# Block-sparse attention with a gated FFN on one core: first keys issued ahead of the constants, the first FFN products split, more zero matmuls at the start, and a new order of all work

## The chip, the cores and the metric

The kernel runs on one core of a Trainium2 chip. The metric is the device time of one execution in microseconds (us), the lower the better. Times are given as the median of several runs; the profile is one further execution, with its own time beside its span from the first to the last instruction. In the text PE is TensorE (PEld its weight loads), ACT ScalarE, DVE VectorE, POOL GpSimd and SP SyncE.

## What is computed

Attention over 4 batches, 8 heads, 768 tokens of 64 values, with a mask of 32 x 32 blocks: the neighbouring blocks, the first and last block row and column, and three sampled blocks per block row. Its output, 3072 tokens of 512 values, goes through a gated feed-forward layer. Cut from the reference:

```python
scores = scale * np.matmul(q, k.transpose(0, 1, 3, 2))
mask = np.abs(blk_i - blk_j) <= window
mask = mask | (blk_i == 0) | (blk_j == 0) | (blk_i == n_blocks - 1) | (blk_j == n_blocks - 1)
for qb in range(n_blocks):
    for kb in sampled_blocks[qb]:
        mask[qb * block:(qb + 1) * block, kb * block:(kb + 1) * block] = True
scores = np.where(mask, scores, -1000000000.0)
...
attn = attn / (np.sum(attn, axis=-1, keepdims=True) + 1e-09)
x = np.matmul(attn, v)      # as (3072, 512)
gate = 1.0 / (1.0 + np.exp(-(x @ w_gate)))
out = gate * (x @ w_val) @ w_out
```

## The kernel before

**Tiling.** A unit is 256 query tokens of one batch: 12 units, three per batch. In a unit the heads go in four pairs, and each pair in three steps of 256 keys. A step is a score (matmuls of kT and qT, 64 rows each, the two heads side by side on the two halves of TensorE's rows), an exp on ACT from PSUM to the tile P (128x1024), and a multiplication of P by the mask on DVE. A pair's value product, PV, multiplies P with the values, which carry a column of ones, so that the row sums come out with it (24 matmuls of 128 rows in the first two units, 48 of 64 rows later); DVE then takes the reciprocal and writes the normalized x. x is turned into xT, in the first two units by TensorE and a copy, later by a DMA transpose on SP's queue.

**FFN.** Units are grouped: the first four groups are one unit each (256 tokens), the later four two each (512). An FFN job computes one PSUM slot full of the gate's and the value's products over four chunks `c` of 128 values, one chunk for each pair of heads; ACT takes a tanh of the gate half, DVE multiplies into `ht`. In the one-unit groups a group has six jobs. Then `y` multiplies `ht` with w_out in parts of four `f` each, and the output goes through a copy and an SP DMA.

**The head.** The first unit's masking is done by adding: extra matmuls of `bias` and the spread matrix `e64` go into each score's PSUM sums, in place of the DVE multiplication. The mask needs the sampled block numbers (`mask_blocks`, task 0), spread by a matmul to rows (tasks 1 to 4; task 2 writes `bias`, task 4 `mb24`), and mask tiles made from `mb24` by matmuls and copies. The first pair's keys and queries are loaded as f32 into `k32` and `q32`, cast on ACT or DVE, transposed by TensorE (tasks 5 to 13: keys in two pieces, 5 to 7 and 8 to 10, and queries, 11 to 13) and copied to `kT` and `qT`. The other pairs' first keys, queries and values, the rest of the queries, and all weights are cast by DMA on POOL's queue in the order of `FIRST`, one after another. Tasks 30, 32 and 34 are the first pair's three scores. The zero matmuls (`idle`, from the tile `junk`) are pairs that read zeros and write a PSUM slot.

**What sets the order.** The schedule is manual. Each piece of work is a task of `Plan` with its engines, estimated costs and dependencies. `Plan.run` goes through the string ORDER: a token is a task's number, with a letter for the engine where there is a choice, `:n` for one of four PSUM slots (each two banks, tiles `m0` to `m3`) that the task takes, and `@n` to let a load wait for a score. `j3` is a pair of zero matmuls into slot 3. The order in the string is the order on every engine and queue; waits come from the data dependencies. Tasks are numbered as they are added, so most numbers after the first FFN job differ between the two kernels.

**Lines** of the profile: L247 and L252 to L257 the first DMAs, L220 and L230, L235 loads and weights, L280 and L282 copies on ACT and DVE, L315 zero matmuls, L338 nearly all matmuls, L397 spread rows, L451 and L456 TensorE transposes, L411 the bias, L570 exps, L576 masks, L615 and L616 the norm, L667 xT transposes by DMA, L762 and L765 tanh and gate.

Of the kernel before, what the change touches and what calls it, by code (L numbers as in the profile page):

```python
# [12 lines left out]
f16 = mybir.dt.float16  # L13
f32 = mybir.dt.float32
# [27 lines left out]
23D 25:3 27:2 37 26D 215@30 50:1 28D 46:3 51 82:2 48:0 83D 47 64:1 49 84:2 60:0 85D 65 38:3 29 61  # L42
56:2 39 66:1 57 42:0 67D 54:3 43D 52:1 165:0 53D 55 93:2 24 58:1 166 94 99:3 59 68:2 95:0 100 96D
181:1 69D 62:0 182 63D 78:3 102:2 162:0 79D 144@102 103 70:1 126:3 125@50 71D 183 163 164 111:1
127 119:2 131:0 120 128 167 112 104 138:3 122:2 132 145:1 123 133 121 139 124 169:0 146 140 147
72:2 170 86:3 159:1 73D 87 171 152:2 160 205:0 153 108:3 88 89:1 206 105@89 90 101 174:2 92@165
154 109 187@89 207 239:1 91 235@86 175 155:0 188:3 110 156 114@40 176 168@155 240 113 115:0 157
189 141:2 116 202:1 142 190 195:0 203 143 196 232:3 172:2 233 129:0 173 97:3 191:2 130 204 192A
193 98A 117:0 256 212:2 194 216 118A 213 184:3 177:0 217 178A 185 134:2 148:0 218 149D 135D 241
242:0 198:3 221A 252:2 214 199 136 179 219A 258 180 246:3 200 253 227 137 254 268:1 247 257 243  # L50
248 150 229:2 234 151 269 209:3 300:0 210 270 259 161 230 237 197 293:1 296:3 228 301 284:2 231
297 302 238 244 294 280:0 186 287:3 285 201@280 211 281 286 249:1 298 288 277:0 223:2 289 278 250
224 251 336:3 327:0 337 158@336 225 274 264:1 279 261:2 271:3 265 295 236 328 262 266 272 310:1
329 273 311 226 263 307:2 320:3 255 340 308 290 312 303:1 321 309 323:2 341 282 324 333:3 208 304
378@333 322 342 334 305 347:2 345A 343D 351:3 314:1 245@351 352 348 338 372:0 315 299@64 349 373
365:3 316 357@181 369 375:2 353 386:0 403@239 358:1 376 317 374 366 387 377 325 354:2 359 367 355
368 404:0 360 356 432:3 400:2 405 433 361 313@400 260 393:1 326@307 401 335 411:3 267@333 406 402
418:2 394 419 424@418 412 407 283@138 395 362:0 413 389:2 379:1 390 414 363 397:3 425:2 364 398
# [3 lines left out]
442:3 385 448 493:2 457A 451 455A 443 371 516:1 465 494 517 444 507:0 429 430 495 518 459:3 490:1  # L62
# [3 lines left out]
532:2 644:0 551 533 529:1 645 534 597:2 562 530 646 563 557 598 594:0 564 578 392@594 595 531  # L66
601:1 633@421 565D 567A 561@32 627:2 569:0 610 628 573:3 579@141 570 602 438@122 571 574 629
339@555 630:2 587:0 631 596 704@50 647:3 575 588 548@397 603 648 604 600@470 580:2 396 683@209 589
662:1 545:3 581 668@165 663 590 632 619:0 546 622:1 664 582 599 620 611:3 623 583 612 621 615:2
624 665:3 625 673:0 666 616 547 350 674 756:1 614@40 634:3 675 757 710 695 584:0 553 617 635 445  # L70
718@435 618 651:1 636 535@662 585 650@102 680:2 652 586 681 637 684:0 653 613 677:2 701:3 654 685
# [3 lines left out]
739:0 727 733 679 731 743:3 740 744 734 741 755 688:1 752 735A 722:0 728 689 737A 723 690 787:3  # L75
749:2 788 724 801:1 572 742 798:0 745 790:3 750 799 748 709 751 791 766:0 541 802 792 769:3 759
770 711 772:1 767 760 773 768 676 844:3 779:0 761 775:1 762A 764D 845 780 763 818:2 776 781 800
# [6 lines left out]
906 916 885 912 909A 921:1 913 974 946 922 924 927 923 907D 970:3 941:2 900 931 971 901:0 942 972  # L84
918:3 932 917 919 933 902 947:2 934D 954:3 936A 975 903 959:0 965:1 960 943 948 961 955 949 966
# [6 lines left out]
1067:0 1065 1081 1068 1085 1069 937 1066 1070 1086 935 1074 910 1075 1087 1076 1090D 1100:3 1091  # L92
1079D 1096:0 1077D 1078 1101 1080 1097 1102 1132:2 1103 1098 1088A 1108:3 1099 1089 1120:1 1109
1112:0 1110 1121 1111 1113 1122 1092:3 1123 1114 1124:1 1115 1133 1093 1104:0 1094 1125 1095 1105
1126 1134 1136:3 1127 1106 1135 1116:1 1107 1128:2 1117 1137 1118 1129 1119 1138 1140:0 1139 1130
1141 1131 1142 1150:1 1151 1152 1143 1153 1144 1154 1145 1160:3 1146A 1148D 1161 1147 1162 1149
1155:2 1163 1156 1164 1157 1158 1159
# [23 lines left out]
class Plan:  # L121
# [33 lines left out]
def kernel(  # L155
# [30 lines left out]
    const_np = np.zeros((128, 128 + 8 * NB), np.float16)  # L186
    const_np[:, 0:128] = np.eye(128)
    const_np[0:NB, 128:] = mc_np.reshape(NB, 4 * NB).view(np.float16)
    const_h = nc.inline_tensor(const_np, name="bb_const")
# [10 lines left out]
    const = sing.tile([128, 128 + 8 * NB], f16)  # L200
    ident = const[:, 0:128]
# [38 lines left out]
    mc = const[0:NB, 128:].bitcast(f32).rearrange("a (n c) -> a n c", c=4)  # L240
# [11 lines left out]
    nc.sync.dma_start(const, const_h.ap())  # L252
# [3 lines left out]
    nc.gpsimd.dma_start(e64[0:NB], spread_h.ap())  # L256
    nc.scalar.dma_start(e64[D : D + NB], spread_h.ap())  # L257
# [55 lines left out]
    def idle(unit):  # L313
# [789 lines left out]
```

## Time and profile before

| | us |
|---|---|
| median of 3 runs | 283.81 (283.0, 283.81, 402.41) |
| profiled execution | 281.96 |
| its span | 280.2 |
| exps on ACT (144) | 142.5 busy, 1.025 each |
| mask multiplications on DVE (132) | 86.7 busy, 0.686 each |
| FFN gate and value matmuls (2 x 672) | 136 busy for each of the two, side by side |
| PV matmuls (2112) | 48.2 busy |

The page gives busy time and counts by engine, the span in 40 slices, the DMA queues, the chain that ended last, and the costliest groups of instructions. Matmuls overlap in TensorE's pipeline, so their busy time is longer than the time between two starts. In the timeline a row gives start, length, engine, line, operation, tiles and count, with the idle time in front of it and what ended it in brackets. The mean granted clock of the profiled execution is 0.994 of full speed.

### The profile page before, as it was taken

To read this page: it belongs to the slowest core of one execution; us is meant where nothing else is said; L and a number is where in the kernel's file an instruction comes from. 1 tells how busy PE (TensorE), PEld (TensorE's weight loads), DVE (VectorE), ACT (ScalarE), POOL (GpSimd) and SP (SyncE) were. 2 spreads that over 40 slices of the span, in tenths; PEclk is the share of its full clock that TensorE was granted. 3 is DMA by queue.
4 is the path that set the end of the run, shared out by engine and by line. 5 is a ranking of instruction groups with operands and counts; after the bars stand their busy time and mean duration, and the time that the engine had idled before them with its cause. 6 is when DMAs were issued, how large, how long until landed. Compare 5 with 4: busy or idle time off the path is not lost.

```text
span 280.2 us, 10875 instructions
## 1 busy us (share of the span) xinstructions
PE 272.4 (97%) x4889; PEld 186.1 (66%) x4889; DVE 187.9 (67%) x387; ACT 192.1 (69%) x239; POOL 47.4 (17%) x70
## 2 busy tenths in 40 slices
PE   5999999999999999999999999999999999999995
PEld 2677786777899799766555655666656667555543
DVE  4667894788887888688778746875664888142421
ACT  3798888699897878898668866578677683023301
POOL 8975441011531000082400000000000000000000
PEclk9799999999999999999999999999999999999999
DMA  7999999765589975279967330041100012440003
GB/s 148 184 195 196 200 205 202 110 127 87 77 110 150 206 129 126 40 106 188 125 115 162 68 97 2 12 133 50 30 2 0 6 21 65 117 180 2 0 5 147
DMA packets 56679, 28.92 MB, mean 103 GB/s; under 512 B 33044, under 2 KB 53676, under 8 KB 56632
## 3 DMA queue, kind: packets, MB, share of 16 engines
q0 software_dynamic: 21552, 13.93, 35.6%
q1 hardware_dynamic: 34592, 13.99, 22.7%
q8 instruction: 38, 0.62, 0.9%
q10 hardware_dynamic: 488, 0.30, 0.4%
q14 instruction: 9, 0.07, 0.1%
HBM read 28.47 MB, written 6.29 MB: 124 GB/s over the span
## 4 chain that ended last, share of the span: by engine, by line
PE 91%; DMA 3%; ACT 2%; DVE 2%; issue 1%; SPq 0%; DVEq 0%
PE m L338 89%; DMA xT<-x 2%; DMA e<-bb_spread 1%; ACT P L570 1%; PE m L456 1%; DVE ysb L833 1%; ACT ysb L831 0%; PE m L451 0%; DVE kT L282 0%; DVE mask L282 0%; ACT mask L280 0%; SPq L667 0%; PE m L397 0%; DVE x L616 0%; PE m L315 0%
## 5 line engine op out<-in xcount | busy, mean ns | idle before, releaser
L570 ACT ACTIVATE P<-m 128x1024 f16<-128x1024 f32 x144 | 142.5, 1025 | 31.3 <-PE m L338 27.3
L338 PE MATMUL m<-xT,wv 64*128 64x512 f16 (+2 forms) x672 | 136.1, 331 | 0.3 <-issue 0.3
L338 PE MATMUL m<-xT,wg 64*128 64x512 f16 (+2 forms) x672 | 135.9, 331 | 0.1
L576 DVE TENSOR_TENSOR P<-P,mask 128x1024 f16<-128x1024 f16 x132 | 86.7, 686 | 11.1 <-ACT P L570 10.8
L338 PEld LDWEIGHTS <-wg 64*128 64x128 f16 (+1 forms) x672 | 61.8, 94 | 20.5 <-issue 2.0
L338 PEld LDWEIGHTS <-wv 64*128 64x128 f16 (+1 forms) x672 | 61.8, 94 | 15.9 <-issue 0.3
L338 PE MATMUL m<-wo,ht 64*128 64x512 f16 (+2 forms) x564 | 70.7, 372 | 0.0
L765 DVE SCALAR_TENSOR_TENSOR ht<-th,m 128x512 f16<-128x512 f32 x72 | 49.0, 686 | 30.6 <-ACT th L762 29.6
L762 ACT ACTIVATE th<-m 128x512 f32<-128x512 f32 x72 | 42.7, 598 | 36.0 <-PE m L338 35.3
L338 PE MATMUL m<-qT,kT 64*128 64x256 f16 x576 | 54.0, 272 | 0.3 <-DVE ysb L833 0.2
L338 PEld LDWEIGHTS <-P 64*128 64x128 f16 (+1 forms) x2112 | 46.2, 94 | 9.0 <-issue 1.1
L338 PE MATMUL m<-vex,P 64*128 64x65 f16 (+1 forms) x2112 | 48.2, 190 | 0.0
L338 PEld LDWEIGHTS <-ht 64*128 64x128 f16 (+1 forms) x564 | 30.5, 94 | 21.6 <-issue 1.3
L338 PEld LDWEIGHTS <-kT 64*128 64x128 f16 x576 | 27.4, 95 | 13.0 <-issue 1.7
L220 POOL DMA_DIRECT2D v<-in_v_dram x16 | 11.4, 717 | 65.3 <-PE m L338 56.5
L616 DVE TENSOR_TENSOR x<-m,rz 128x256 f16<-128x256 f32 x48 | 20.4, 425 | 1.7
L615 DVE RECIPROCAL rz<-m 128x4 f32<-128x4 f32 x48 | 8.7, 180 | 17.9 <-PE m L338 16.4
L220 POOL DMA_DIRECT2D q<-in_q_dram x19 | 13.6, 723 | 12.1 <-PE m L338 11.1
L831 ACT ACTIVATE ysb<-m 128x512 f32<-128x512 f32 x13 | 7.5, 597 | 10.6 <-PE m L338 9.9
L833 DVE TENSOR_SCALAR ysb<-m 128x512 f32<-128x512 f32 x9 | 6.1, 688 | 11.8 <-ACT ysb L831 5.5
L220 POOL DMA_DIRECT2D k<-in_k_dram x15 | 10.8, 723 | 6.1 <-PE m L338 5.5
L338 PE MATMUL m<-bias,e 64*128 64x256 f16 x48 | 6.9, 301 | 0.3
(46 smaller groups left out, 69.7 us busy)
## 6 DMA issues: line engine op xcount, KB each, us to landing
out_dram<-ysb SPq DMA_DIRECT2D x23, 256.0 KB, 2.4
v<-in_v_dram POOLq DMA_DIRECT2D x16, 192.0 KB, 5.5
k<-in_k_dram POOLq DMA_DIRECT2D x15, 192.0 KB, 5.9
q<-in_q_dram POOLq DMA_DIRECT2D x12, 192.0 KB, 7.1
wg<-in_moe_w_gate_dram POOLq DMA_DIRECT2D x6, 256.0 KB, 8.6
wv<-in_moe_w_val_dram POOLq DMA_DIRECT2D x6, 256.0 KB, 8.9
wo<-in_moe_w_out_dram POOLq DMA_DIRECT2D x3, 512.0 KB, 12.8
xT<-x SPq DMA_TRANSPOSE x40, 3.2
```

Source lines behind the costliest of these rows:

```text
L220: return nc.gpsimd.dma_start(dst[:, h0:h1, t0:t1, :], src[b, h0:h1].rearrange("h (p t) d -> p h t d", t=NT)[:, :, t0:t1, :],)
L338: return nc.tensor.matmul(out, lhsT, rhs, start=start, stop=stop, skip_group_check=True).ins
L456: nc.tensor.transpose(out16[a * D : (a + 1) * D, h, i * D : (i + 1) * D], tile_[rows, a], ident[rows, rows],)
L570: nc.scalar.activation(self.pt.rearrange("a h i n -> a (h i n)"), both(self.bank).rearrange("a h n -> a (h n)"), AF.Exp, bias=0.0, scale=SCALE
L576: nc.vector.tensor_tensor(self.pt, self.pt, m.unsqueeze(1).broadcast_to([128, 2, 2, UQ]), op=ALU.mult,)
L615: nc.vector.reciprocal(rz, self.acc[:, :, :, D : D + 1])
L616: nc.vector.tensor_tensor(self.x16.rearrange("a s h d -> a h s d"), self.acc[:, :, :, 0:D], rz.broadcast_to([128, 2, 2, D]), op=ALU.mult,)
L762: nc.scalar.activation(th, both(bank)[:, 0, :], AF.Tanh, bias=0.0, scale=0.5)
L765: nc.vector.scalar_tensor_tensor(self.ht[:, tiles[0] : tiles[-1] + 1, :], in0=th.rearrange("a (f n) -> a f n", n=self.w), scalar=1.0, in1= ...
L831: nc.scalar.activation(ysb, both(bank)[:, s, :], AF.Copy, bias=0.0, scale=0.5)
L833: nc.vector.tensor_scalar(ysb, in0=both(bank)[:, s, :], scalar1=0.5, scalar2=None, op0=ALU.mult)
```

## The change

Four things.

1. The constants. Identity and block table were one tensor `const` (128 x 320, 80 KB), loaded first on SP's queue. They become `ident` (128 x 128, 32 KB) and `mc` (24 x 24 x 4, f32, 9 KB). SP's queue issues now keys, identity, and the spread rows for partitions 0 to 23; ACT's queue block table, sampled blocks, queries; POOL's queue first the spread rows for partitions 64 to 87.
2. The first two jobs of the first group's FFN are two tasks each: chunks 0 to 2, which wait for three pairs' xT, and chunk 3, which waits for the fourth's.
3. Zero matmuls: tokens `j1s` and the like are pairs with 128 columns instead of 512. The head has 10 wide pairs and 4 narrow ones; it had 8 wide ones.
4. ORDER is new from beginning to end: the order of all tasks, their PSUM slots, the engines of the copies with a choice, and the scores that the loads wait for. The first pair's keys are cast by ACT (first piece) and DVE (second), its queries by ACT; task 32 is the first score instead of task 30; the mask tiles come after it.

```diff
+EARLY = 2
 ORDER = """
-j3 j3 j3 j3 0 j3 j3 j3 11D 1:0 8A 3:1 5D 12:2 6:3 4A 7D 2 13A 80:3 106:1 9:0 30:2 107A 10D 81D
-15:1 31 34:0 16D j3 76:3 17:2 35 32:1 18D 77D 74:2 33 40:0 14 20:3 75D 41 44:1 21D 22:2 45 19 36:0
...
+j3 j3 j3 j3 0 j3 j3 j3 5A 8D 1:0 j1 11A 6:1 2 j2s 9:2 12:3 3:0 10D 13A 7A j2s 32:2 4D j3 15:3 33
+j1s 78:1 34:0 16D 79A j3s 80:3 30:2 81D 35 17:1 18D j3 76:3 31 20:1 77D 40:0 21D 22:3 41 36:2 19
+97:1 23D 37 44:0 98D 50:3 45 27:1 46:2 28D 25:1 51 48:0 26D 24 47 54:1 49 74:3 55 75D 60:0 64:2 14
+61 66:3 58:1 67D 65 56:3 59 117:0 57 118D 86:1 89:2 29 68:0 90 38:3 69D 87 93:0 39 62:2 52:3 94
+102:1 63A 103 42:2 53D 95:0 43D 108:3 96D 111:2 109 70:0 104 126:1 71D 112 110 119:3 88 140:0 127
+120 113 132:2 128 141 129 130:3 72:1 131 122:0 133 91 147:3 134 73D 123 135 142 84:1 99:2 148
...
             if token[0] == "j":
-                self.idle(int(token[1:]))
+                self.idle(int(token[1]), 128 if token[2:] else 512)
...
-    const = sing.tile([128, 128 + 8 * NB], f16)
-    ident = const[:, 0:128]
+    ident = sing.tile([128, 128], f16)
...
-    mc = const[0:NB, 128:].bitcast(f32).rearrange("a (n c) -> a n c", c=4)
+    mc = sing.tile([NB, NB, 4], f32)
...
-    nc.sync.dma_start(const, const_h.ap())
+    nc.scalar.dma_start(mc, mc_h.ap())
     nc.scalar.dma_start(sbi, sampled_blocks)
     first_heads(nc.sync, k32, k, 0, NT)
     first_heads(nc.scalar, q32, q, 0, 2)
-    nc.gpsimd.dma_start(e64[0:NB], spread_h.ap())
-    nc.scalar.dma_start(e64[D : D + NB], spread_h.ap())
+    nc.sync.dma_start(ident, ident_h.ap())
+    nc.sync.dma_start(e64[0:NB], spread_h.ap())
+    nc.gpsimd.dma_start(e64[D : D + NB], spread_h.ap())
...
-    def idle(unit):
+    def idle(unit, n):
         for i in range(2):
             nc.tensor.matmul(
-                units_ps[unit][:, i, :],
+                units_ps[unit][:, i, 0:n],
                 junk[i * D : (i + 1) * D, 0:128],
-                junk[i * D : (i + 1) * D, :],
+                junk[i * D : (i + 1) * D, 0:n],
...
+            if self.g == 0 and j < EARLY:
+                a = plan.add(
+                    [(PE, 1.5 * F_HALF)],
+                    half(None, range(3)),
+                    xdone[0][:3] + before("ht", 0),
+                    take=bank,
...
+                a = plan.add(
+                    [(PE, 0.5 * F_HALF)],
+                    half(None, range(3, 4)),
+                    [a] + xdone[0][3:],
...
-            if self.ns[-1] < WIDE:
+            elif self.ns[-1] < WIDE:
```

In the new order task 126 is the first part of the first FFN job and task 103 the exp that uses its PSUM slot before; 63 is the copy of a pair's xT that ACT makes, 79 a mask tile's copy on ACT, 70 transposes of later queries. In the old order task 126 is the first FFN job whole.

More of the change, by code (lines that the diff above doesn't have):

```diff
@@ L45 @@
[L45 to L56, printed above, removed]
@@ new lines @@
+270:1 139 216 221A 236 223A 153 202 167:3 271 231:2 229 302:0 232 181 239 230 272 168 233 197:2
+241:1 182 169 254:3 198 195 303 196 199 260 248:2 255 304 240 242 258 256 259 266:0 243 249 251:1
+225:3 267 250 252 261 226 253 106:2 273:0 107A 227 309:1 276 274 310 114@309 207:2 275 312:3
+247@46 208 313 292 295:0 286:1 209 296 268 297 263:3 287 279:2 289:0 203@263 238 264 288 160@143
+280 228 265 298:1 290 329:3 299 291 325:2 330 163 326 281 322:0 282:1 314 331 323 262 305:2 283
+300 356:0 342 311 357 338:1 257 343 327 339 353:0 284 344 354 380@353 210 306 359@143 347D 345A
@@ new lines @@
+391:1 367:0 269@56 392 307 316:3 324 328@36 335:2 402:1 340 317 341@99 336 368 318 405@183 403 337
+420:2 332 381:3 358 369 364:1 421 319 370 382 393 365 383 349:0 366 413:2 384 350 399:1 427:3 351
+400 426@399 404 374:0 394@399 414 355 375 315@244 401 437:1 428 415 285@30 422 438 360:0 301@122
+416 429 448:1 444:2 430 449 361 277 406:3 376 362 432 465:1 363 445 433 466 407 446 395:0 333 224
+408 434:1 371 441:2 435 409 396 293 385 377:3 439 442 378 320 472:1 222 397 443 321 473 379 388:3
+423:0 467 454 389 278 455 424 390 334 451:1 450 518:3 410:0 452 436 456 417 425 519 478:1 308 457A
@@ new lines @@
+453 411 479 459A 412 475:3 431 461:2 480 482:0 476 481 462 483 463 468:1 485:3 469 484 471 521:2
[4 rows of a table added]
+398 533 557:3 597 566 589:2 558 567D 571:1 569A 562 610:3 590 352 611 559 616@108 603:0 591 580
+706@30 632:3 592 572 440@30 633 604 598 670@560 586:2 573 605 652@46 621:3 587 606 635@50 700:1
+622 701 588 624:0 550@560 623 685@157 629:2 682:1 582:3 630 581@231 625 537@489 683 631 613:2 634
+583 626 684 614 617:1 627 584 703:2 664:0 585 618 665 447 636:3 612 720@282 704 653:0 563@89 619
+602@231 599:2 620 637 600 555 717:1 712 556 654 638 615 718 639 657:2 570 666 655 675:3 667:1 656
[4 rows of a table added]
@@ new lines @@
+751:2 791 729 752 730 745:1 753 662 746 644 698 820:3 645 736 821 761 595 739D 731:1 737D 784:3
+732 833 748:0 762 747 749 733 771:1 785 772 776 800:0 822 763 786 773 801 813:1 750 766A 856:0
+764D 814 767 787 663 857 815 768:2 858 810:3 699 769 816 792:0 811 770 793 777:1 740 757 803:2
[4 rows of a table added]
+889 861 900:2 920:3 678 906 901 864 849:0 890 921 907 893 850 917:2 908 913:3 911A 909D 897:0 914
+918 848 923:1 851 898 915 903:2 924 904 899 869:3 932 916 972:0 964:2 919 925 973 926 905 870 965
+946:0 902 933 947 871 940:2 974 887 961:3 934 962 922 1018:0 941 1006:3 935 1019 942 960 953:2
@@ new lines @@
+1007 936D 967:0 938A 937 954 1049:3 939 968 955 1050 971 1021:1 995:2 1022 956:3 969 1031:1 970
[6 rows of a table added]
+1078 1089 1081D 1102:3 1079D 1080 1094:0 1106:1 1095 1107 1096 1090A 1103 1097 1092D 1098:0 1104
+1093 1108 1114:2 1105 1082 1099 1115 1100 1118:3 1101 1116 1109 1126:0 1117 1110:1 1122:2 1111
+1119 1112 1127 1113 1120 1123 1128 1130:1 1129 1124 1121 1134:0 1125 1138:3 1135 1139 1136 1131
+1137 1140 1142:2 1141 1132 1143 1133 1144 1157:0 1145 1146 1147 1162:3 1150A 1163 1148A 1151 1158
+1091 1164 1149 1159 1165 1152:1 1160 1166 1161 1153 1154 1155 1156
@@ L185 @@
     )
[L186 to L189, printed above, removed]
+    ident_h = nc.inline_tensor(np.eye(128).astype(np.float16), name="bb_ident")
+    mc_h = nc.inline_tensor(mc_np, name="bb_blocks")
     spread_h = nc.inline_tensor(e24_np, name="bb_spread")
@@ L355, in turns, with whole @@
                 )
-    def whole(mms, bank):
+    def whole(mms, bank, begins=True, ends=True):
         for n, job in enumerate(mms):
@@ L361, in whole @@
                 out, lhsT, rhs = job(g, slice(0, 128))
-                bank.last = tiled(out, lhsT, rhs, n == 0, n == len(mms) - 1)
+                bank.last = tiled(
+                    out, lhsT, rhs, begins and n == 0, ends and n == len(mms) - 1
+                )
     copies = {}
@@ L740, in f, with half @@
             tiles = range(self.per * j, self.per * (j + 1))
-            def half(first):
+            def half(first, cs=range(4)):
                 def go(eng):
@@ L745, in go @@
                     for o, f in enumerate(tiles):
-                        for c in range(4):
+                        for c in cs:
                             mms.append(
@@ L754, in go @@
                     if first is None:
-                        whole(mms, bank)
+                        whole(mms, bank, cs[0] == 0, cs[-1] == 3)
                     else:
@@ L774, in f @@
             deps = xdone[self.g] + before("ht", self.g)
-            if self.ns[-1] < WIDE:
+            if self.g == 0 and j < EARLY:
[4 more added lines that the diff above has]
+                    take=bank,
+                    ops=12 * self.per,
+                    wide=True,
+                )
+                a = plan.add(
+                    [(PE, 0.5 * F_HALF)],
+                    half(None, range(3, 4)),
+                    [a] + xdone[0][3:],
+                    ops=4 * self.per,
+                    wide=True,
+                )
+            elif self.ns[-1] < WIDE:
                 a = plan.add(
```

27 lines of the change are left out of this document (4 added, 23 removed), and 39 rows, old and new, of the table ORDER.

## The prediction

> **What bounds the kernel now.** I read the page first, then busy time by stretches, then the head in the timeline and the DMA issues.
>
> ```profile
> PE 272.4 (97%) x4889; PEld 186.1 (66%) x4889; DVE 187.9 (67%) x387; ACT 192.1 (69%) x239; POOL 47.4 (17%) x70
> ```
>
> TensorE is busy 97% of the span, so only the work that it waits for, or does slowly, can be gained. The stretches say where that is (busy us and count for PE, PEld, DVE, ACT, POOL, then the granted clock and DMA):
>
> ```profile
> 0.00:10.00 10.00, 6.74 (x81) 3.36 (x81) 4.87 (x16) 5.00 (x7) 8.55 (x16) 0.92 0.92 156
> 10.00:20.00 10.00, 9.65 (x226) 7.00 (x226) 6.89 (x17) 8.73 (x10) 8.15 (x12) 0.91 1.41 195
> 20.00:30.00 10.00, 9.77 (x170) 7.17 (x165) 7.33 (x18) 9.17 (x12) 6.07 (x9) 1.00 1.45 195
> ...
> 240.00:250.00 10.00, 10.00 (x96) 5.46 (x94) 3.19 (x6) 1.58 (x3) 0.00 (x0) 1.00 0.50 173
> ```
>
> Busy time overlaps in the pipeline, so I count by pitch, from start to start in the timeline: 0.108 us for a 64x512 matmul (two run side by side), 0.109 for 128x256, 0.0545 for 64x256, 0.015 for 64x65, 0.030 for 128x65. By these, the work that starts before the first FFN matmul (25.02) is 12.0 us: 13.0 are lost there. From 25.02 to 50.23, where the second group's FFN begins, work is 23.4 of 25.2: 1.85 lost. From 50.23 to the last output tiles (269.64) only 3.6 of 219.4 are lost. The gain is to be sought in the head.
>
> What paces the head is ScalarE's chain of exps. Timeline of ScalarE and, by single microseconds, the clock:
>
> ```profile
> 5.28 0.62 ACT L280 CAST qp<-kp 128x512 f16<-128x512 f32 x1 [3.26 <-DMA kp<-in_k_dram]
> ...
> 8.08 1.02 ACT L570 ACTIVATE P<-m 128x1024 f16<-128x1024 f32 x1
> 9.55 1.02 ACT L570 ACTIVATE P<-m 128x1024 f16<-128x1024 f32 x1 [0.45 <-PE m L338]
> 11.41 7.67 ACT L570 ACTIVATE P<-m 128x1024 f16<-128x1024 f32 x8 [0.84 <-DVE mask L282]
> ...
> 22.78 3.77 ACT L570 ACTIVATE P<-m 128x1024 f16<-128x1024 f32 x4 [0.20 <-PE m L338]
> ```
> ```profile
> 8.00:9.00 1.00, 0.88 (x32) 0.74 (x32) 1.00 (x3) 1.00 (x2) 1.00 (x2) 0.72 1.37 188
> 9.00:10.00 1.00, 1.00 (x10) 0.33 (x6) 0.23 (x1) 0.55 (x2) 0.99 (x2) 0.50 1.40 190
> ...
> 11.00:12.00 1.00, 1.00 (x14) 0.67 (x10) 1.00 (x3) 0.58 (x1) 1.00 (x3) 0.58 1.41 174
> ```
>
> The first exp starts at 8.08; the 15th ends at 24.72 and frees the PSUM slot that task 70's transposes take, and behind them the first FFN matmul stands (25.02). Fifteen exps at 0.96 (8 in 7.67) are 14.4 of these 16.6 us; ScalarE stood idle 2.0, of which 1.3 (0.45 and 0.84) in a stretch, 8.44 to 11.84, in which the granted clock was 0.5 and pairs of 64x256 came 0.21 apart instead of 0.11.
>
> **Keys in front of the constants.**
>
> ```profile
> kp<-in_k_dram SPq DMA_DIRECT2D x1, 384.0 KB, 4.1
> ...
> kp<-in_q_dram ACTq DMA_DIRECT2D x1, 128.0 KB, 4.0
> ...
> const<-bb_const SPq DMA_DIRECT2D x1, 80.0 KB, 2.0
> e<-bb_spread POOLq DMA_DIRECT2D x1, 36.0 KB, 4.0
> ```
>
> The keys were issued at 1.15 and landed at 5.25; now they take SyncE's first place (0.74): 4.85. The queries go from ScalarE's second place to its third (1.40 to 1.86, where that queue issued its third DMA before). Their landing lies between 5.4, as now, if the bytes in flight set it (the 80 KB constant gives way to 41 KB), and 5.86 by their own 4.0. The block numbers move from 0.77 to some 1.4, which delays the mask blocks (done 3.66) to 4.3, still before anything that needs them. The spread rows for partitions 0 to 23 go behind the identity on SyncE: between 3.6 (issue 1.6 and the constant's 2.0) and just behind the keys, 5.3; the half that stays on GpSimd landed at 5.58 and keeps its place. GpSimd's later loads move past nothing.
>
> The first score now: query cast on ScalarE (0.38 to 0.48), four transposes (0.2), query copy 0.38 beside the mask-row matmuls (three, 0.59), four bias and four key matmuls (0.62 to the last end): 1.6 after the queries, 7.0 to 7.5. I take 7.2; outer bounds 6.9 and 7.7. The key path (DVE cast 0.68, transposes 0.3, bias 0.41, copy 0.42) is done by 6.7, under it.
>
> **The head to the first FFN matmul.** Its slot is freed by the 15th exp again, task 103, but in the chain stand now a mask copy (0.59), which was done ahead of the first exp, and an xT copy (0.38), which DVE did. 7.2 + 15 x 0.96 + 0.06 + 0.97 = 22.6, matmul at 22.65: 2.35 earlier. This takes ScalarE as never idle. Scores cost TensorE 0.44 per exp, some 0.25 of transposes and masks beside: under 0.96 at full clock. The loads allow it: the last keys and queries of the head landed by 12.8, needed at about 15. If ScalarE keeps half of its old idle, 1.0 is lost again.
>
> **First FFN jobs in two parts.** The same 16 matmuls; the first 12 need three pairs instead of four. The fourth pair's transposes stand ahead of them in the new order anyway, so this hides at most one copy (0.29) and a 0.4 matmul tail; it is in the 22.65. Behind the second part's wait for that copy stands the second job, but the copy ends under the first part's 1.3.
>
> **Zero matmuls.** 16 become 20 of 512 columns and 8 of 128: two pairs at 0.216 and four at some 0.055 more, 0.65 in all. They lie in waits for ScalarE, and cost nothing while those last; without the cover 0.65, at half clock 1.3.
>
> **FFN and weights.** From the first FFN matmul to the third part of the first y stand, in the new order, six FFN jobs (10.5), two y parts (1.7), 12 scores (2.6), four PVs (2.8) and 0.45 of transposes and a mask: 18.1, so 40.9 with 0.2 of waits. The weights come by GpSimd's queue at the old times, as DMA runs at 195 GB/s without a break: the last wv (issued 24.01, 9.8) at 33.8, needed at 34.8; the third wo (27.98, 13.5) at 41.5, needed at 40.9. TensorE waits 0.6 there. With these two waits and 0.1 after, 0.9 is lost from the first FFN matmul to the second group's, against 1.85: a gain of 0.95. The next batch's keys and queries (first one issued at 28.96, landing in 13.4) have about 1.4 to spare.
>
> **The other orders.** ScalarE, DVE and the matmul count stay; after 50 us the 3.6 lost can fall to 2 or rise to 6. At two places the new order leaves 4.3 and 4.5 us of TensorE work between a pair's last PV matmul and the FFN job that reads its xT (at some 116 and 202 us), where 6.05 was the least: 0.3 for both. Sum: 2.35 + 0.95 - 0.3 = 3.0. The profiled execution took 281.96, 280.2 of it span: 277.2 and 279.0. The runs before have 283.0 and 283.81 beside a stray 402.41; from the median, **280.8**.
>
> The half clock lasted from 8.44 to 11.84 (shares 0.72 and 0.58 of its first and last microsecond), and the longest idle time of TensorE ahead of it was 0.8. [...]
>
> **Rivals.** (1) The half clock comes in spite of the fillers. For it: it came when TensorE was busy 38 to 91% of each microsecond from 5 to 8, and from 4.85 to about 5.6 it will be idle still. Against: fillers stand now between the transposes. Price: ScalarE's 1.3 us of idle time return: 282.1. Chance 0.2.
> (2) The first score comes no earlier: queries and spread rows land where they did or later, as they stand third. Price: the 0.9, 281.7. For: keys and queries landed within 0.2 of each other. Chance 0.1.
> (3) Slower: xT lands too late at the two short places. From PV to issue it takes 0.75 (DVE's 0.18 and 0.42 with gaps), from issue to landing 3.2 in the median, 5.9 at most (SyncE's xT transposes). It decides from 3.6. At 5.9 both stall by 2.3: with the 0.3 returned, 285.1. For: 5.9 occurs, where loads are in flight. Against: in the new order the last batch's loads go only after the first of these jobs, and none is left at the second; the median suffices. Chance 0.09.
> Forecast 0.58; 0.03 for what I don't see.
>
> **Numbers.** Low end: gain of 3.0, and 1.6 off the later losses, and the runs' 0.8 spread: 278.4. High: rival 1, with 1.7 of new losses later: 283.8; rival 3 is left out. Two per cent, 5.7 us, is about what a measurement of this kernel can tell from no change: faster by that needs 278.1 or less, 0.07; slower by that needs rival 3 with more places than two, 0.03; within, 0.9.
>
> **What would show it.** First exp at 7.2 (6.9 to 7.7), ScalarE without idle time to 22, clock 1.00 from 5 to 30, first FFN matmul at 22.65, a wait for wo near 41, equal losses after 50. A clock of 0.5 near 9 is rival 1; waits of TensorE near 116 and 202 for xT are rival 3. I am wrong if the losses after 50 us grow by more than 2.

## The result, and the profile after

The change made the kernel slower: 287.57 us in the median of its runs (285.51 to 291.94) beside 283.81 of the kernel before, a ratio of 1.0131 with a 95% interval of 1.0095 to 1.0167. That is under the 2% that a single comparison is trusted with, so "no change by 2%" was right, but it is a loss, and the forecast was a gain: 280.8, with a range that ended at 283.8. One run of each kernel (402.41 before, 291.94 after) was in a slow state, and the ratio leaves both out.

The profiled execution after took 286.93, 285.2 of it span. I count "lost" time as in the prediction: span less the work that starts in it, by its pitch (zero matmuls are no work). The work is the same in both kernels, so the totals, 27.06 for 22.09, differ by as much as the spans do, and the table says where:

| | before | after | all four repairs (e10) |
|---|---|---|---|
| first exp starts | 8.08 | 8.93 | 7.79 |
| first FFN matmul | 25.02 | 25.77 | 24.50 |
| lost up to 50 us | 14.71 | 15.64 | 14.34 |
| lost 50 to 100 | 2.06 | 5.16 | 2.85 |
| lost 100 to 270 | 1.61 | 1.90 | 2.07 |
| lost 270 to the end | 3.70 | 4.35 | 3.74 |

The page's line of engines and, with one row added, the same stretches in the profile after (busy us and count for PE, PEld, DVE, ACT, POOL, then the granted clock and DMA), and behind them the added stretch in the profile before:

```profile
PE 274.3 (96%) x4901; PEld 190.9 (67%) x4901; DVE 187.5 (66%) x387; ACT 190.8 (67%) x239; POOL 47.4 (17%) x70
```
```profile
0.00:10.00 10.00, 7.39 (x77) 3.79 (x79) 3.93 (x14) 3.76 (x6) 8.62 (x17) 1.00 0.93 155
10.00:20.00 10.00, 9.36 (x221) 6.89 (x218) 6.81 (x16) 9.04 (x11) 8.15 (x12) 1.00 1.41 195
20.00:30.00 10.00, 9.65 (x195) 7.67 (x192) 7.70 (x19) 9.33 (x12) 5.18 (x7) 1.00 1.45 197
83.00:93.00 10.00, 7.75 (x176) 7.37 (x172) 6.85 (x15) 6.73 (x8) 3.52 (x5) 1.00 0.91 133
240.00:250.00 10.00, 10.00 (x158) 5.77 (x154) 2.75 (x7) 0.09 (x1) 0.00 (x0) 1.00 0.36 81
```
```profile
83.00:93.00 10.00, 9.72 (x234) 8.50 (x228) 8.00 (x18) 8.29 (x10) 2.28 (x4) 1.00 1.10 147
```

The surprise is the fourth row: from 83 to 93 us, deep in the steady part, TensorE is busy 7.75 of 10 us (9.72 before). The clock of 1.00 in the first row is not to be believed: the first clock record of this execution is at 11.09, and pairs of 64x256 stand 0.21 apart until then and 0.11 behind it, as at the granted 0.50 and 1.00 of the profile before: half speed.

**The head.** DMA issues of the first 9 us, then ScalarE's timeline, both after:

```profile
kp<-in_k_dram SPq DMA_DIRECT2D x1, 384.0 KB, 3.2
kp<-in_q_dram ACTq DMA_DIRECT2D x1, 128.0 KB, 4.6
```
```profile
4.00 0.40 ACT L280 CAST qp<-kp 128x256 f16<-128x256 f32 x1 [1.99 <-DMA kp<-in_k_dram]
6.54 0.40 ACT L280 CAST qp<-kp 128x256 f16<-128x256 f32 x1 [2.13 <-DMA kp<-in_q_dram]
...
8.93 1.02 ACT L572 ACTIVATE P<-m 128x1024 f16<-128x1024 f32 x1 [0.95 <-PE m L338]
10.25 0.58 ACT L280 CAST mask<-m 128x512 f16<-128x512 f32 x1 [0.30 <-PE m L338]
11.11 1.94 ACT L572 ACTIVATE P<-m 128x1024 f16<-128x1024 f32 x2 [0.27 <-PE m L338]
13.48 10.42 ACT L572 ACTIVATE P<-m 128x1024 f16<-128x1024 f32 x11 [0.44 <-PE m L338]
24.09 0.37 ACT L280 COPY xT<-m 128x256 f16<-128x256 f16 x1 [0.18 <-PE m L453]
24.50 2.85 ACT L572 ACTIVATE P<-m 128x1024 f16<-128x1024 f32 x3
```

The keys did land earlier (3.98 for 5.25), but the queries, now third on ScalarE's queue, were issued at 1.90 and landed at 6.51 (5.41 before). The first exp starts 0.85 later than before. From there to the end of the 15th exp it takes 16.59 us, as before (16.64): of the old 2.0 of idle time 0.95 is now filled by the mask copy and the xT copy, and the rows' brackets still leave 1.2.

**The new gaps.** TensorE's timeline after at 61 us, and the chain that ended last (start, length, what) near 85 and 92; then the one such row of TensorE's timeline before:

```profile
60.65 0.37 PE L338 MATMUL m<-vex,P 64*128 64x65 f16 x13
61.58 0.70 PE L338 MATMUL m<-vex,P 64*128 64x65 f16 x35 [0.56 <-issue]
```
```profile
85.09 0.61 ACT th L764
85.70 0.89 issue
86.59 5.27 PE m L338 x128
91.86 0.65 issue
92.51 2.49 PE m L338 x62
```
```profile
83.83 0.27 PE L338 MATMUL m<-xT,wv 64*128 64x256 f16 x1 [0.28 <-issue]
```

At 61 TensorE stops in the middle of one PV's products, and "issue" means that it waited for nothing that the profile shows. At 85 the profile puts the first part of the stop down to a tanh (85.09 to 85.70) and only the 0.89 behind it to "issue". The tanh did not hold the score, though: in e5 below, which has the same order of work, the same score starts ahead of that tanh:

```profile
84.58 0.40 PE L337 MATMUL m<-qT,kT 64*128 64x256 f16 x4
```
```profile
84.75 0.60 ACT L763 ACTIVATE th<-m 128x512 f32<-128x512 f32 x1
```

So the whole stop, from 84.72 to 86.59, has no cause on another engine that the profile shows. Between the stops at 85 and 92 lie exactly 128 matmuls (`x128`). Each matmul comes with a weight load (4901 of each on the page), so 128 matmuls are 256 instructions. The page has a DMA queue that fits: 38 packets of instructions with 0.62 MB, 16 KB each, and 2 x 4901 TensorE instructions are 38.3 times 256. By these counts the packets carry TensorE's own instructions, 256 in each, and the three gaps (0.72, 1.76 and 0.81 above the pitch, 3.3 together; before there is one of 0.44, at 83.3) stand where it steps from one such block into the next. When the block for the stop at 85 came, the DMA answers for the stretches 80.7 to 83.4 and 83.4 to 84.9 of the kernel after tell (packets, MB, share of 16 engines):

```profile
q0 software_dynamic: 517, 0.37, 93.6%
```
```profile
q0 software_dynamic: 17, 0.01, 6.4%
q8 instruction: 1, 0.02, 5.9%
```

TensorE entered the block in hand at 80.66. In the 2.8 us behind it the queue of the key, query and value loads (q0) held the 16 DMA engines for 93.6% of the time, and no instruction packet moved; the one packet came at 83.48 to 84.89, and TensorE went on at 86.59. The loads in flight here are a burst of six, issued 0.7 apart at 73.98 to 77.58, the last of which landed at 85.79. A second burst of five, at 83.33 to 86.11, lies over the next block: TensorE entered that one at 86.59, its packet moved 3.69 later (90.28 to 91.25), and the stop at 92 followed.

**The end.** The last step of the chain before, then after:

```profile
277.00 0.42 DVE ysb L876
```
```profile
281.45 0.69 DVE ysb L894
```

The new order puts the full 128x512 output last, before it was a half tile. From the last matmul's end to the span's end it takes 3.75 for 3.24.

### The profile page after: what moved, and what is told of

Its sections match the earlier page's. It is cut to its first block, busy times and chain, and to the rows that moved or that the text cites. A ratio compares the mean times of both kernels' runs of the same rounds, so it can differ in the third digit from the quotient of the medians.

```text
span 285.2 us, 10906 instructions
## 1 busy us (share of the span) xinstructions
PE 274.3 (96%) x4901; PEld 190.9 (67%) x4901; DVE 187.5 (66%) x387; ACT 190.8 (67%) x239; POOL 47.4 (17%) x70
## 4 chain that ended last, share of the span: by engine, by line
PE 88%; DVE 4%; DMA 3%; ACT 2%; issue 1%; ACTq 0%; DVEq 0%
PE m L338 86%; DMA kp<-in_q_dram 2%; DMA xT<-x 1%; DVE P L578 1%; ACT P L572 1%; PE m L458 1%; DVE x L618 1%; PE m L315 1%; DVE mask L282 0%; ACT th L764 0%; DVE ysb L851 0%; PE m L453 0%; DVE rz L617 0%; DVE ht L767 0%; DVE ysb L894 0%
## 5 line engine op out<-in xcount | busy, mean ns | idle before, releaser
L338 PE MATMUL m<-qT,kT 64*128 64x256 f16 x576 | 55.0, 271 | 1.9 <-ACT th L764 1.6
L338 PEld LDWEIGHTS <-P 64*128 64x128 f16 (+1 forms) x2112 | 45.3, 94 | 7.7 <-issue 0.9
L338 PE MATMUL m<-vex,P 64*128 64x65 f16 (+1 forms) x2112 | 46.8, 190 | 0.6 <-issue 0.6
L338 PEld LDWEIGHTS <-ht 64*128 64x128 f16 (+1 forms) x564 | 31.7, 94 | 20.6 <-issue 1.5
L338 PEld LDWEIGHTS <-kT 64*128 64x128 f16 x576 | 29.0, 95 | 15.8 <-issue 4.3
L851 DVE TENSOR_SCALAR ysb<-m 128x512 f32<-128x512 f32 x10 | 6.7, 688 | 11.2 <-PE m L338 8.4
L849 ACT ACTIVATE ysb<-m 128x512 f32<-128x512 f32 x12 | 6.9, 606 | 6.2 <-PE m L338 5.6
L315 PE MATMUL m<-junk 64*128 64x512 f16 (+1 forms) x28 | 6.7, 515 | 1.8 <-DVE junk L286 1.7
```

Source lines behind the costliest of these rows:

```text
L315: nc.tensor.matmul(units_ps[unit][:, i, 0:n], junk[i * D : (i + 1) * D, 0:128], junk[i * D : (i + 1) * D, 0:n], start=True, stop=True,)
L338: return nc.tensor.matmul(out, lhsT, rhs, start=start, stop=stop, skip_group_check=True).ins
L849: nc.scalar.activation(ysb, both(bank)[:, s, :], AF.Copy, bias=0.0, scale=0.5)
L851: nc.vector.tensor_scalar(ysb, in0=both(bank)[:, s, :], scalar1=0.5, scalar2=None, op0=ALU.mult)
```

## The experiments

All ratios are to runs of the kernel before on the same chip; line numbers shift by a few from kernel to kernel. Theories: *instructions* (the loss lies where TensorE's own instructions arrive late), with *operands* as its rival (the loads' bytes or other waits of the new order hold the work back); and for the head *landing* against *exps* and *clock*.

**e1: fewer instructions.** The PV of all units from the third on with 12 matmuls of 128 rows per half instead of 24 of 64 rows, 960 matmuls fewer in all:

```diff
-            for s in range(2):
+            for s in (0, 1) if first is None else (0,) if first else (1,):
...
-            if first is None:
-                whole(mms, self.bank)
-            else:
-                turns(mms, self.bank, first)
+            whole(mms, self.bank, first is not False, first is not True)
```

> The changed kernel; from the third unit on, each half of a PV is 12 matmuls of 128 rows in place of 24 of 64 rows. Same work at the same pitch by row (0.030 against 2 x 0.015), 960 TensorE matmuls and as many weight loads fewer. Theory A (TensorE waits for its own instructions: 16 KB blocks, 128 matmuls each, that are fetched late while loads of keys and values are in flight): the gaps put down to issue at 61, 85 and 92 us (0.7, 1.8, 0.8) shrink to under 0.5 in sum, and the profiled execution is 2.5 to 3.5 us shorter. Theory B (those gaps are waits for ScalarE, PSUM slots or xT that the new order made): they stay within 0.5 us, the time too.

Measured: 295.26, ratio 1.0428 (1.04 to 1.0456). The gaps at 61, 85 and 92 are gone, which agrees with instructions, yet the time rose. TensorE's timeline in e1 shows why:

```profile
101.06 0.27 PE L338 MATMUL m<-xT,wv 64*128 64x256 f16 x1
101.26 0.54 PE L338 MATMUL m<-vex,P 128*128 128x65 f16 x12
101.73 0.28 PE L338 MATMUL m<-xT,wv 64*128 64x256 f16 x1
```

From the last 64-row matmul to the first of 128 rows it is 0.20 where the pitch is 0.109, and the twelve take 0.47 where twelve pitches are 0.36: 0.09 is lost going in and 0.11 coming out. From 62 to 260 us there are 115 such changes, some 11.5 us at 0.1 each, which is more than the 3.3 of the stops. As a test of instructions by the time this run is spoilt; it measured something else of use, below.

**e2: the loads without their bytes.** The third batch's loads bring 2 of 128 partitions.

```diff
-                lambda eng: load_heads(dst, src, b, 2 * p, 2 * p + 2),
+                lambda eng: load_heads(dst, src, b, 2 * p, 2 * p + 2)
+                if b != 2
+                else nc.gpsimd.dma_start(
+                    dst[0:2, 2 * p : 2 * p + 2],
+                    src[b, 2 * p : 2 * p + 2].rearrange("h (p t) d -> p h t d", t=NT)[0:2],
+                ),
```

> The changed kernel; the loads of the third batch's keys, queries and values bring 2 of 128 partitions only (the rest of that batch's data is left out, so its results are those of other data). All instructions, waits and their order stay. Theory A: the instruction fetches from 70 to 95 us start without delay, the gaps at 85 and 92 us vanish (2.5 us less); the one at 61 us, ahead of most of these loads, may stay. Theory B: the gaps stay.

Measured: 285.07, 1.0059 (1.0032 to 1.0086). The gaps at 85 and 92 are gone, the one at 61, where no such load is in flight, stayed (0.85). The instruction packets themselves show the link: behind TensorE's entry into the blocks ahead of the stops at 85 and 92 they start after 0.10 and 0.16 us in e2, after 2.80 and 3.69 in the change. The loads cause two of the three.

**e3 and e4: the two halves of the change.** e3 is the kernel before with the constants and first DMAs of the change; e4 is the changed kernel with those of the kernel before (part 1 of the change and its reverse).

```diff
...
-    nc.sync.dma_start(const, const_h.ap())
+    nc.scalar.dma_start(mc, mc_h.ap())
     nc.scalar.dma_start(sbi, sampled_blocks)
     first_heads(nc.sync, k32, k, 0, NT)
     first_heads(nc.scalar, q32, q, 0, 2)
-    nc.gpsimd.dma_start(e64[0:NB], spread_h.ap())
-    nc.scalar.dma_start(e64[D : D + NB], spread_h.ap())
+    nc.sync.dma_start(ident, ident_h.ap())
+    nc.sync.dma_start(e64[0:NB], spread_h.ap())
+    nc.gpsimd.dma_start(e64[D : D + NB], spread_h.ap())
```

> The kernel before with the changed kernel's constants and first DMAs alone, old order. If the late queries (landing 6.5 against 5.4) cost what they delay: first exp about 9.0 to 9.2 against 8.08, and 0.8 to 1.2 us slower than before. Rival, that ScalarE's idle time takes it up: within 0.3 of before.

> The changed kernel's order, split products and fillers, with the constants and first DMAs of before. Queries land at 5.4 again: first exp at 7.8 (at half clock) to 7.3 (full clock), the first FFN matmul 1.1 earlier than in the changed kernel (25.8), and the time about 1 us under the changed kernel's; the gaps from 60 to 95 us stay, so it is still 1 to 3 us slower than before. If the late DMAs are the whole cause, it is as fast as before or faster.

Measured: e3 283.93, 1.0043 (1.0014 to 1.0073); e4 286.28, 1.0113 (1.0087 to 1.014). Of 283 us that is 1.2 for the DMAs and 3.2 for the order; together 1.56% where the whole change has 1.31% (0.95 to 1.67). In e3 the queries landed at 6.81 and the first exp started at 9.97 (at half speed until 11.03, which the expected 9.0 to 9.2 left out). In e4 they landed at 5.17, and still the new order won nothing in the head (at half speed until 10.86):

```profile
8.35 1.02 ACT L574 ACTIVATE P<-m 128x1024 f16<-128x1024 f32 x1 [0.95 <-DVE mb L284]
...
12.99 10.38 ACT L574 ACTIVATE P<-m 128x1024 f16<-128x1024 f32 x11 [0.52 <-PE m L340]
```

15th exp done at 25.02, first FFN matmul at 25.26: 0.24 later than before. And the old order is not free of the stops: e3 has 1.05 at 84.8 and 0.80 at 91.0, where the profiled run of before had 0.44 and none.

**e5: the same loads, spread.** Eleven load tokens of ORDER stand behind other scores, most of them 2 to 4 us apart:

```diff
-380@353 ... 359@143 ... 269@56 ... 328@36 ... 341@99 ... 405@183 ... 426@399 ... 394@399 ... 315@244 ... 285@30 ... 301@122
+298:1 269@298 ... 322:0 426@322 ... 338:1 328@338 ... 391:1 285@391 ... 402:1 315@402 ... 420:2 301@420
+... 399:1 380@399 ... 437:1 359@437 ... 448:1 405@448 ... 434:1 394@434 ... 388:3 341@388
```

> The changed kernel with the eleven loads of the third batch behind other scores of the second unit, about 2 us apart and each from about 7 us earlier to 11 us later than now; all bytes are still brought, and nothing else moves. Instruction theory (TensorE's own next 16 KB of instructions wait behind five loads issued 0.7 us apart): the two gaps at 85 and 92 us (1.76 and 0.81) shrink below 0.5 together while the one at 61 us (0.72) stays; time 287.57 - 2.2 = about 285.3. Load theory (the bytes themselves, wherever they are put, hold TensorE's operands back): the 2.5 us only move with the loads; time 287 to 288, the gaps at other places and in front of matmuls that wait for a tile.

Measured: 284.58, 1.0082 (1.0053 to 1.0112). The stretch of 83 to 93 us in e5:

```profile
83.00:93.00 10.00, 10.00 (x241) 9.17 (x238) 8.38 (x18) 8.42 (x11) 2.80 (x4) 1.00 0.82 88
```

TensorE is busy all 10 us (7.75 in the change) with all bytes brought; the gaps at 85 and 92 went together and came nowhere else (lost from 80 to 100: 0.24 for 2.71), the one at 61 stayed at 0.87. That is instructions against operands. The burst matters, not the bytes: in the change six and then five loads of 192 KB were issued 0.7 apart, in e5 two of the eleven stand that close and the rest 2.0 to 4.2 apart. The instruction packets of the two blocks start 1.66 and 1.79 behind TensorE's entry, between the 0.1 to 0.2 of e2 and the 2.8 to 3.7 of the change, and that is soon enough.

**e6: the run of PVs broken up.** In the change eight PV halves stand almost back to back at 59 to 61 us, and 128 matmuls are used up in 2.24 us. One FFN job (286) goes in between:

```diff
-... 253 106:2 273:0 107A 227 309:1 276 274 310 ... 295:0 286:1 209 ...
+... 253 227 106:2 286:1 107A 287 276 273:0 288 274 309:3 310 ... 295:0 209 ...
```

> The changed kernel with the run of eight products with the values at 59 to 61 us broken up: one FFN job (16 long matmuls) is put in front of the last four, and the scores behind take other banks. Instruction theory: 128 matmuls there take 4 us instead of 2.24, so the gap of 0.72 at 61 us goes; the gaps at 85 and 92 stay; time 286.5 to 287.0. Rival (the gap at 61 is the fill of the products' pipeline or a wait that the records do not show): the gap moves along with the products and stays 0.7; time 287.5.

Measured: 288.13, 1.0197 (1.0145 to 1.025): not the gain in time that was expected, but the gap went as the instruction theory has it. At the same instruction 0.23 is left, so it was the block and not the products. Of the other two stops, which were expected to stay, the one at 85 did (1.7, now at 88.7), the one at 92 did not. But the job that I moved had been covering others, which now wait for their PSUM slots: 0.43, 0.35 and 1.01 at 61 to 67.7 us. This execution also has its clock at half until 13.75, which made its head 1 us longer.

**e7: queries first.**

```diff
-    nc.scalar.dma_start(mc, mc_h.ap())
-    nc.scalar.dma_start(sbi, sampled_blocks)
     first_heads(nc.sync, k32, k, 0, NT)
     first_heads(nc.scalar, q32, q, 0, 2)
+    nc.scalar.dma_start(mc, mc_h.ap())
+    nc.scalar.dma_start(sbi, sampled_blocks)
```

> The changed kernel with the first queries in front of the block constants and the sampled blocks on ScalarE's queue. Landing theory (the first exp is late because the queries were issued at 1.90 and took until 6.51): queries issued at about 0.8 land at 4.5 to 5.4, the first exp starts at 7.2 to 8.0 instead of 8.93, the 15th ends at 24.0 to 24.6 instead of 25.52 and the whole kernel takes 286.6 to 286.9. Rival (the landing is set by the bytes of keys, queries and loads together, whatever the place in a queue): queries land after 6, first exp after 8.6, time 287.5. If the sampled blocks land too late for the mask blocks, the first biased score moves instead and the first exp is the only thing that gets earlier.

Measured: 286.26, 1.014 (1.0074 to 1.0206): the time cannot tell it from the change. The trace can. Issues in e7, where the queries were issued at 0.77 and landed at 4.44:

```profile
kp<-in_k_dram SPq DMA_DIRECT2D x1, 384.0 KB, 3.5
kp<-in_q_dram ACTq DMA_DIRECT2D x1, 128.0 KB, 3.7
```

First exp 8.33, 15th done 24.77, first FFN matmul 25.01: 0.76 earlier than in the profile of the change, not the 1.5 and more that the landing offered. A part even of this is the clock, which was at full speed from 4.95 in e7: with the change's own first DMAs and full speed from 5.5 to 6.0, e1, e2 and e5 have that matmul at 25.54, 25.55 and 25.28. So queries first are worth 0.3 to 0.5. The sampled blocks, now last on that queue, were converted at 5.28 instead of 4.27, and the mask row behind them took over.

**e8: no zero matmuls.** All `j` tokens of ORDER are left out, 14 pairs.

```diff
-j3 j3 j3 j3 0 j3 j3 j3 5A 8D 1:0 j1 11A 6:1 2 j2s 9:2 ...
+0 5A 8D 1:0 11A 6:1 2 9:2 ...
```

> The changed kernel without its zero matmuls; the order is otherwise kept. If the zero matmuls do what the clock needs (they bring full speed sooner than without them), the clock is released later than 11.1 us, the head's short matmuls stay at half speed longer, and the time is 288 to 289. If the release of the clock is not in their hands and the exps set the head's pace, the first FFN matmul stays at 25.5 to 26.0 and the time at 287.2 to 287.9.

Measured: 290.14, 1.0265 (1.0207 to 1.0323), 2.6 us above the change by the medians. The clock in e8 by single microseconds:

```profile
26.00:27.00 1.00, 1.00 (x29) 0.54 (x25) 0.79 (x3) 1.00 (x2) 1.00 (x2) 1.00 1.45 196
27.00:28.00 1.00, 1.00 (x14) 0.72 (x7) 1.00 (x3) 1.00 (x2) 0.50 (x2) 0.56 1.45 197
28.00:29.00 1.00, 1.00 (x6) 0.67 (x5) 1.00 (x3) 0.49 (x1) 0.56 (x1) 0.50 1.44 203
```

Full speed came at 13.47, and a second half-speed stretch lay at 27.12 to 30.53, just when the FFN starts. The longest idle time of TensorE in the 4 us ahead of it is 0.90. The loss is not the clock's alone. The mean clock of e8's four executions is 0.994, 0.994, 1.00 and 1.00, and the two at 1.00 took 289.11 and 289.8, still longer than the change's median. In the profiled one the stops at block boundaries add up to some 5.3 us, 2 more than in the change. So the kernel without zero matmuls is slower, but how much of that is the clock, and whether zero matmuls hold the clock up, is not shown.

**e9: the old end.** The full tile's tasks (1152 to 1156) go ahead of the half tiles'.

```diff
-1144 1157:0 1145 1146 1147 1162:3 1150A 1163 1148A 1151 1158 1091 ... 1152:1 1160 1166 1161 1153 1154 1155 1156
+1144 1152:0 1153 1154 1091 1145 1155 1146 1156 1147 1162:3 1150A 1148D 1151 1163 ... 1157:1 1165 1158 1166 1159 1160 1161
```

> The changed kernel with its last three outputs in the order of the kernel before: the full 128x512 tile ahead of the two half tiles, so that the last eviction is 128x256. Eviction theory: from the last matmul's end to the span's end it takes 3.2 us as before instead of 3.75 (eviction 0.42 for 0.69, half the bytes to store); time 287.57 - 0.5 = 287.0. Rival (the store's fixed latency makes the tail, whatever is stored): the tail stays at 3.7 and the time at 287.5. If an eviction now waits behind the two of the unit before, the gain is eaten there.

Measured: 287.16, 1.0152 (1.0109 to 1.0195); the time does not resolve half a microsecond here, the trace does. Last step of the chain in e9:

```profile
282.42 0.43 DVE ysb L893
```

From the last matmul to the end 3.16 instead of 3.75. Over all kernels run, those that end with the full tile have 3.72 to 3.79, those that end with the half 3.16 to 3.24.

**e10: all four repairs on the change.** e5's loads; the FFN job of e6 with slots that are free by then; keys and queries first, the sampled blocks second on SyncE's queue; e9's end.

> The changed kernel with four repairs: the third batch's loads spaced as in e5; the run of products at 59 to 61 us broken up by one FFN job as in e6, but with banks that are free by then; queries and keys first in their queues with the sampled blocks second on SyncE's; the last outputs in the order of e9. If the losses are what the single runs showed and they add: -3.0 (spaced) -0.7 (products) -0.8 to -1.3 (queries, blocks) -0.5 (tail) from 287.57 = 282 to 282.6, beside 282.8 to 283.8 of the kernel before. Rival (what is repaired in one place comes back in another, since the instruction fetch only meets other transfers): 284 to 285.

Measured: 284.1, 1.0041 (1.0013 to 1.007). About 2.5 of the 3.7 us came back by the ratios, and the losses are in the last column of the table above; the kernel before was not reached. Two new waits are larger than the 0.9 by which its profiled span is longer than before: 0.68 for a slot at 63.3, and 0.69 for a turned query tile at 102.3, whose load I had put too late.

**e11 and e12: the kernel before, with its loads spread.** The same cure for the old order, nine loads behind other scores; e12 has e10's first DMAs besides.

```diff
+357@310 ... 267@320 ... 283@333 ... 326@375 ... 313@354 ... 403@400 ... 378@418 ... 424@397 ... 299@421
```

> The kernel before with nine of its third batch's loads behind other scores, about 2 us apart instead of in bursts of five; nothing else. Instruction theory: its own stall at 83.3 us (0.44 in the profiled run, and 1.05 + 0.80 at the same two boundaries where only its head was moved, in e3) goes: 0.4 to 1.8 faster than before, 281.2 to 282.6. Rival (before was never held by its loads): ratio 0.998 to 1.002.

> e11 with the constants in parts and the first keys and queries in front of everything on their queues, the sampled blocks second on SyncE's queue, the block constants second on ScalarE's. Landing theory: queries land at 4.4 to 4.8 instead of 5.41 and the sampled blocks by 4.4, first exp at 7.2 to 7.7 instead of 8.08; the 15 exps behind keep their pace: 0.4 to 0.9 faster than e11, 280.5 to 282. Rival (exps and copies in the head, not the landing, set when the FFN starts): same as e11 within 0.3.

Measured: e11 282.28, ratio 0.9955 (0.9924 to 0.9986), the only kernel here that is faster than the kernel before by its whole interval, though by less than 2%; e12 282.2, 0.9984 (0.9955 to 1.0012), no gain beside it. In e11 0.11 is lost from 80 to 90 us (0.52 before). In e12 the queries landed at 4.36, but the first exp started at 8.31 (8.15 in e11): in the old order the mask row stands ahead of it, and the blocks, converted at 4.60, feed it no earlier. Landing was not what the old head waits for. (Behind the first exp the two can't be compared: e12 ran at half speed from 8.31 to 11.73, e11 at full speed from 5.36 on.)

## Why the prediction was wrong

The forecast was 3.0 shorter, and the profiled span is 4.97 longer. Of these 8.0 us, some 3.1 lie ahead of the first FFN matmul, 1.1 from there to 50 us, and 3.75 behind.

**First exp at 7.2 (bounds 6.9 to 7.7): failed, 8.93.** The step "their landing lies between 5.4 and 5.86" did. Issued third at 1.90 rather than 1.86, which was right, the queries took 4.6 and not 4.0 us: the bound took the old duration for the longest, though the keys, the spread rows and GpSimd's loads are in flight for all of it. Six executions with this head have the landing at 6.5 to 7.3. (The mask blocks, too, were done later than forecast, at 5.1 for 4.3, but still ahead of what needed them.) Behind the landing came 2.42 to the first exp where I had 1.6. That is the clock: of the six, the three that are at half speed then took 2.41 to 2.42, the three that are not 1.72 (e1, e2, e5). So 0.9 of the miss is the landing and 0.8 the clock. The part of the clock is luck of the profiled execution; the landing is not. Rival 2 was right here, and too mild: it gave "no earlier", and it was 0.85 later.

**"This takes ScalarE as never idle": failed.** 1.23 of idle time is left beside the 0.95 of copies. It is not the clock: in e10, at full speed from 4.61 on, the chain to the 15th exp takes 16.45, in the change 16.59. (In e10 two of TensorE's stops at block boundaries, 0.2 and 0.5 long, lie in that chain.) Instead of 2.35 earlier the first FFN matmul came 0.75 later; in e10, with the landing put right, it comes 0.52 earlier than before, and 0.25 earlier than in e11, which has the old order and was at full speed too.

**0.95 from there to the second group's FFN: failed, nothing.** 1.74 was lost before (the prediction's rougher sum had 1.85), 1.71 after, 1.71 in e10. There was no wait for the third wo part. The loss that I wanted to save was no waiting at all: 14 changes between 64-row scores and 128-row FFN matmuls lie in that stretch in both kernels, and at the 0.1 each that e1 makes plain (1.4 in all) they are most of it. The new order did not change their number.

**0.3 for two short xT places: right.** One wait of 0.32 at 211 us, none at 116. Rival 3 did not happen.

**Equal losses after 50 us: the step that failed most**, and the one I had named as what would make me wrong. Losses grew by 3.10 up to 100 us, by 0.3 to 270, by 0.65 behind. Of the 3.10, 2.85 are the three stops for instruction blocks less the one of before. I had weighed orders by their waits for data; what the order also sets is how soon 256 instructions are used up, and which loads are in flight when the next block is due. That these stops are fetches that loads delay is shown for two of the three (e2, e5); for the one at 61 us it is shown that it stands at a block boundary and goes when the block lasts longer (e6, e10). The 0.5 at the end, the full tile last, could have been read from the last tokens of ORDER and was not looked at.

**Rival 1 (half clock in spite of the fillers): it came, and cost half of its price.** Six executions have this very head (the change, e1, e2, e5, e6, e9); the clock was released at 5.45, 5.47, 6.01, 11.09, 11.09 and 13.75. From the first exp to the first FFN matmul they took 16.7 to 17.1, and 17.75 in the last. So half speed until 11 cost nothing behind the first exp, where I had priced 1.3, but the 0.7 ahead of it; until 13.75 it cost 0.7 and about 1 more. With one head, then, the release came anywhere from 5.45 to 13.75; in the profile of before the clock changed at 5.02, 8.43 and 11.84, 3.41 us apart. In e8 a half-speed stretch followed on idle times of 0.9 at most. That fillers keep half speed away, as the forecast of a clock of 1.00 from 5 us on took it, was my assumption, and no run shows it; whether they can is open: three of the change's own six executions in the ratio have a mean clock of 0.992 to 0.994, and 3.41 us at half speed take 0.006 off the mean.

**What stays open.** The stops differ from run to run in kernels with the same order (0.72 to 1.77 at 61 us), so a part of the 1.31% is chance of this kind: in these two the block's packet started 0.40 and 1.27 behind TensorE's entry into the block ahead (the change and e9). Why TensorE goes on only 1.3 to 1.7 us after the block's packet has landed is not shown. A cure for the stop at 61 us that brings no new wait for a slot was not found: e10 still has one.

## What to carry to other kernels

Before calling a kernel bound by one engine's work, look for its stops that wait for nothing, and count instructions between them: a distance of a whole number of 256s, within two, such as the 256 between the stops at 85 and 92, pointed at the engine's own code here. Bulk loads that are not issued in bursts cured two such stops here without a new loss; breaking up a run of short matmuls cured the third, but brought other waits. When an order is laid out anew, check four things that a list of data waits leaves out: what is in flight at each moment, how fast instructions are used, how often the row size of matmuls changes, and which tile ends the kernel. A DMA put ahead of another can delay that other one by more than its own issue: issued at 0.77 (e7), 1.40 (before) and 1.90 (after), the queries landed 3.7, 4.0 and 4.6 later.

## What the runs showed of the hardware

- TensorE's instructions arrive in blocks of 256 (38 packets of 16 KB for 2 x 4901 in the change) and can stop it. Kernels with different orders stop at the same instruction numbers: with matmuls counted from the first, they stand at numbers 223, 351, 990, 1501, 1629 and 2268, which are 128 apart or a multiple of it (less one where the multiple is 4 or 5). e8, which has 28 matmuls fewer in its head, stops at 351, 990, 1501 and 1629 as well, and so at other work than the change. Sizes: 0.2 to 1.8 us.
- Most steps from one block into the next pass without a stop: the change has 38 packets and three stops over 0.7 between blocks, before has 38 and one of 0.44. Where bursts of five or six loads were in flight, or 128 matmuls passed in 2.24 us, TensorE stopped; all stops between blocks together took 0.4 to some 5.3 us per kernel (before and e8).
- A change between 64-row and 128-row matmuls costs about 0.1 us in either direction (0.09 and 0.11 in e1's rows; 115 changes in e1, 14 in the FFN's first stretch).
- The half-speed state came back, from 27.12 to 30.53, after 4 us in which TensorE was never idle for more than 0.90 us (e8).
